# Linear attention into a sine-gated feed-forward layer: where the attention output products stand, how batch 2's q is transposed, and how the last output block is cut

## The chip, the cores and the metric

The kernel runs on one core of one Trainium2 chip. The metric is the device time of one execution in microseconds (us). A core has a matrix engine (PE, with its weight loads shown as PEld), a vector engine (DVE), a scalar engine (ACT), a general engine (POOL) and a sync engine (SP), which here only issues DMAs. Each engine works through its own instructions in order; engines wait for one another by semaphores. Matrix products land in PSUM, and DVE or ACT must copy a result out ("evict" it) before its PSUM tile can be used again.

## What is computed

Attention without a score matrix: q is a softmax over the head dimension, k a softmax over the sequence, and the output of a head is q times (k transposed times v). The result, 4608 tokens of 512 numbers, goes through a layer with 2048 hidden units.

```python
# q, k, v: (8 batches, 8 heads, 576 tokens, 64)
q_s = softmax(q, axis=-1)
k_s = softmax(k, axis=2)
kv  = einsum('bhsd,bhse->bhde', k_s, v)
x   = einsum('bhsd,bhde->bhse', q_s, kv)      # then to (4608, 512)
h   = x @ w_in                                # (4608, 2048)
s   = sin(alpha * h)
g   = h + s * s / (alpha + 1e-09)
out = g @ w_out                               # (4608, 512)
```

## The kernel before

**Two tilings.** Attention goes by batch: 8 batches of 576 tokens, each token index cut into 9 groups (J = 9) of 64 (P). The layer goes by token tiles of 512: 9 tiles, numbered t = 0 to 8. Tile t + 1 needs tokens of batch t + 1 at the latest, so the attention of batch t + 1 is done while tile t is worked, for t = 3 to 6; batch 3 is done while tile 2 is worked. "Stage t" below is the loop over the 16 hidden blocks ni of tile t.

**The layer.** `mm_h` (L235) makes one hidden block: four products (ki = 0 to 3) over the 512 inputs into a PSUM tile hp, 128 x 512. `sine` (L241 to L247) takes the sine on ACT and the square on ACT, POOL or DVE, by a letter in a string. `combine` (L251) writes g on DVE and frees hp. `o_stream` is a generator: each `take(os, n)` issues n products g x w_out (L255) of the tile before, 64 for a tile, 16 for each of four output blocks; after each 16 `evac_o` copies the block (L261) and stores it in two halves (L264).

**The attention of a batch.** exp of q and k on ACT (L114), row sums on DVE (L136, L137), the division on POOL or DVE, into qn (L143); qn is transposed into qT by a DMA on SP (`q_transpose_dma`, L202). `kv_mm` (L154) makes the 64 x 64 products of k and v with 36 small products, `kv_norm` (L164, L167) divides them on DVE into kbd. `attn_out(b, ii, half, pool, eng)` multiplies kbd with qT for one half ii of the heads and one part of the token groups (groups 0 to 3, or 4 to 8): two products (L212) into one tile xp, and one copy (L215) into xT, the input of `mm_h`. Four calls of it make a batch. Calls are counted 0 to 3 below, in the order (ii 0, first part), (ii 0, second part), (ii 1, first part), (ii 1, second part).

**PSUM.** From stage 2 on: ps_h has four tiles (hp), ps_o two (op, lent to hp in stage 2), and ps_a one, which kvp and xp share. So in ps_a each product waits until the tile's last content was copied out.

**The order.** All is written out by hand in the order of issue; nothing is moved by a scheduler. In stages 2 to 6 `attn_back(b, ni - 5)` is called once a block: at ni = 5 it makes kv, at ni = 10, 11, 12, 13 one call of attn_out each. In stage 2 the copies alternate between ACT and DVE and the combine lags two blocks behind; in stages 3 to 6 the copies are all on DVE and `q_transpose_dma` stands at ni = 4, behind it on SP the stores of the output blocks. `load_batch` queues the q, k and v loads of a later batch on SP.

**Batch 2** is done before stage 2, among the output products of tile 1. Its q is transposed in two DMAs, one for each ii. Its products are made in another form: four products of six token groups (`attn_chunk`, L220), each into a tile of ps_h, and four of three groups into one tile of ps_a; the six groups are the 384 tokens that tile 2 needs. The copies (L440, L445) are two on ACT and three on DVE.

**The tail.** The last output block is made in two parts of 256 columns (L498), each copied on DVE and stored in two halves, one from SP's queue and one from ACT's.

Of the kernel before, what the change touches and what calls it, by code (L numbers as in the profile page):

```python
# [15 lines left out]
F32 = mybir.dt.float32  # L16
# [7 lines left out]
def kernel(  # L24
# [14 lines left out]
    nc = tc.nc  # L39
    ctx.enter_context(nc.allow_non_contiguous_dma(reason="layout"))  # L40
    B, H, S, D = q.shape
    dm = H * D
    d_ff = moe_w_in.shape[1]
    NT = B * S
    J = 9
    P = S // J
    nN = d_ff // 128
    MF = 512
    nT = NT // MF
# [17 lines left out]
    xT = singles.tile([128, 4, NT], BF16, name="xT")  # L67
    win = singles.tile([128, 4, d_ff], BF16, name="win")
    wout = singles.tile([128, nN, dm], BF16, name="wout")
# [6 lines left out]
    def src_view(t, b):  # L76
        return t[b].rearrange("(i e) (p j) d -> (e p) i (j d)", e=2, j=J)
# [7 lines left out]
    def load(name, t, b, halves=False, eng=nc.sync):  # L85
        st = stage.tile([128, 4, J, D], F32, name=f"st_{name}", tag="st")
        view = src_view(t, b)
        flat = st.rearrange("p i j d -> p i (j d)")
        if halves:
            for ii in range(2):  # L90
                eng.dma_start(out=flat[:, ii::2], in_=view[:, ii::2])
        else:
            eng.dma_start(out=flat, in_=view)
        staged[name, b] = st
# [15 lines left out]
    A = {}  # L110
# [14 lines left out]
    def cast_v(b, engs):  # L125
        vv = vb[b % 2].rearrange("p j (i c) -> p i j c", i=4)
        for ii in range(2):
            engs[ii](vv[:, 2 * ii:2 * ii + 2, :, 0:D], staged["v", b][:, ii::2])  # L128

    def norm_q(b, engs):  # L130

        qe = A["qe", b].rearrange("p j (ii x d) -> p ii j x d", ii=2, x=2)
        A["qn", b] = qn = att1.tile([128, 2, J, 2 * D], BF16, name="qn")
        qs = small.tile([128, J, 4], F32, name="qs")
        if len(engs) == 1:
            nc.vector.tensor_reduce(qs, A["qe", b].rearrange("p j (i d) -> p j i d", i=4), axis=AXL.X, op=ALU.add)  # L136
            nc.vector.reciprocal(qs, qs)  # L137
        for ii in range(2):
            part = qs[:, :, 2 * ii:2 * ii + 2]
            if len(engs) == 2:  # L140
                nc.vector.tensor_reduce(part, qe[:, ii], axis=AXL.X, op=ALU.add)
                nc.vector.reciprocal(part, part)
            engs[ii % len(engs)].tensor_tensor(qn[:, ii].rearrange("p j (x d) -> p j x d", x=2), qe[:, ii],  # L143
                                               part.unsqueeze(3).to_broadcast([128, J, 2, D]), op=ALU.mult)
# [27 lines left out]
    def q_tile(b):  # L172
        if ("qT", b) not in A:
            A["qT", b] = att2.tile([128, 2, J, 128], BF16, name="qT")
        return A["qT", b]
# [15 lines left out]
        for j in range(j0, j1):  # L191
            nc.tensor.transpose(tp[:, j - j0], A["qn", b][:, ii, j], identb)

    def q_transpose_dma(b, halves=False):
        for ii in range(2) if halves else (slice(0, 2),):
            out, in_ = q_tile(b)[:, ii], A["qn", b][:, ii]
            if not halves:
                out, in_ = out.rearrange("p ii j c -> p (ii j) c"), in_.rearrange("p ii j c -> p ii (j c)")
                in_ = in_.rearrange("p ii c -> p (ii c)")
            else:  # L200
                in_ = in_.rearrange("p j c -> p (j c)")
            nc.sync.dma_start(out=out, in_=in_, transpose=True)  # L202

    XO = ((0, 4), (4, 9))

    def attn_out(b, ii, half, pool, eng):
        qT, kt = A["qT", b], kbd[b % 2]
        j0, j1 = XO[half]
        n = (j1 - j0) * P
        xp = pool.tile([128, 2, 512], F32, name="xp", tag="a")  # L210
        for e in range(2):
            nc.tensor.matmul(xp[:, e, 0:n], kt[:, e, ii], qT[:, ii, j0:j1, e * 64:(e + 1) * 64],  # L212
                             start=True, stop=True)
        c0 = (J * b + j0) * P
        eng(xT[:, 2 * ii:2 * ii + 2, c0:c0 + n], xp[:, :, 0:n])  # L215

    def attn_chunk(b, c, j0, j1, xp):

        ii, e = divmod(c, 2)
        nc.tensor.matmul(xp, kbd[b % 2][:, e, ii], A["qT", b][:, ii, j0:j1, e * 64:(e + 1) * 64],  # L220
                         start=True, stop=True)


    G = {}
# [29 lines left out]
    def mm_o(t, j, ni, acc):  # L254
        nc.tensor.matmul(acc, G[t][:, ni, j * 128:(j + 1) * 128], wout[:, ni, :],  # L255
                         start=(ni == 0), stop=(ni == nN - 1))

    def evac_o(t, j, acc, eng, cols=None, queues=None):
        cols = cols or slice(0, dm)
        o = opool.tile([128, dm], F32, name="o")  # L260
        eng(o[:, cols], acc)  # L261
        for hf in range(2):
            blk = t * BPT + 2 * j + hf
            (queues or (nc.sync, nc.sync))[hf].dma_start(out=out_v[blk // J, blk % J][:, cols],  # L264
                                                         in_=o[64 * hf:64 * hf + 64, cols])


    ACT_CP, DVE_CP, GP_CP = nc.scalar.copy, nc.vector.tensor_copy, nc.gpsimd.tensor_copy
# [6 lines left out]
    for ii, j0, j1 in VJ:  # L275
        nc.sync.dma_start(out=st[:, ii::2, j0:j1].rearrange("p i j d -> p i (j d)"),
                          in_=src_view(v, 0)[:, ii::2, j0 * D:j1 * D])
# [48 lines left out]
    ps_h = ctx.enter_context(tc.tile_pool(name="ps_h", bufs=4, space=PSUM, reuse_waits="tile"))  # L326
# [5 lines left out]
    def flush(lag, keep):  # L332
        while len(lag) > keep:
            combine(*lag.pop(0))

    def o_quad(t, accs, engs):

        R = range(4)
        orders = [[(n, m) for p in (0, 2) for n in R for m in (p, p + 1)],
                  [(n, m) for n in R for m in R], [(n, m) for n in R for m in R],  # L340
                  [(n, m) for m in R for n in R]]
        for c in R:
            for n, m in orders[c]:
                mm_o(t, m, 4 * c + n, accs[m])
                if c == 3 and n == 3:
                    evac_o(t, m, accs[m], engs[m])
                yield

    def take(it, n=1000):
        for _ in range(n):  # L350
            if next(it, 0) == 0:
                return
# [4 lines left out]
    with tc.tile_pool(name="ps_e", bufs=2, space=PSUM, reuse_waits="tile") as ps_e:  # L357
# [4 lines left out]
        for ni in range(nN):  # L362
            h_slot(0, ni, "PAPDPAPADPAPPDAP"[ni], lag, lent)
            flush(lag, 1)
            if ni in late:
                name, x, b, hv = late[ni]
# [12 lines left out]
        os = o_quad(0, accs, [DVE_CP, ACT_CP, DVE_CP, ACT_CP])  # L379
# [24 lines left out]
    ps_o = ctx.enter_context(tc.tile_pool(name="ps_o", bufs=2, space=PSUM, reuse_waits="tile"))  # L404
    ps_a = ctx.enter_context(tc.tile_pool(name="ps_a", bufs=1, space=PSUM, reuse_waits="tile"))


    def o_stream(t, eng=DVE_CP):
        for j in range(4):
            acc = ps_o.tile([128, dm], F32, name="op", tag="o")  # L410
            for ni in range(nN):
                mm_o(t, j, ni, acc)
                if ni == nN - 1:
                    evac_o(t, j, acc, eng)
                yield
# [4 lines left out]
    os = o_stream(1)  # L420
# [2 lines left out]
    exp_q(3)  # L423
    exp_k(3)
    load("v", v, 3)
    q_transpose_dma(2, halves=True)
    cast_v(3, [GP_CP, GP_CP])
    nc.scalar.activation(zero, zero, AX.Sin)
    take(os, 16)
# [1 line left out]
    kv_mm(2, 1, ps_a)  # L431
    kv_norm(2)
    norm_q(3, [GP])
    take(os, 20)

    c0 = J * 2 * P
    for c in range(4):
        xp = ps_h.tile([128, MF], F32, name="hp", tag="h")[:, 0:6 * P]
        attn_chunk(2, c, 0, 6, xp)
        (ACT_CP, DVE_CP)[c % 2](xT[:, c, c0:c0 + 6 * P], xp)  # L440
        take(os, 1)
    xp = ps_a.tile([128, 2, 512], F32, name="xp", tag="a")[:, :, 0:6 * P]
    for c in range(4):
        attn_chunk(2, c, 6, 9, xp[:, c // 2, (c % 2) * 3 * P:(c % 2 + 1) * 3 * P])
    DVE_CP(xT[:, :, c0 + 6 * P:c0 + 9 * P].rearrange("p (h c) n -> p h c n", h=2),  # L445
           xp.rearrange("p h (c n) -> p h c n", c=2))
    take(os)
    q_transpose_dma(3)
    load_batch(4)

    def attn_back(b, n, engs=(DVE_CP, DVE_CP)):
        if n == 0:
            kv_mm(b, 0, ps_a)
            kv_mm(b, 1, ps_a)
            kv_norm(b)
        elif 5 <= n < 9:
            attn_out(b, (n - 5) // 2, (n - 5) % 2, ps_a, engs[n % 2])

    def lent():
        return ps_o.tile([128, MF], F32, name="op", tag="o")  # L460
# [2 lines left out]
    for ni in range(nN):  # L463
        h_slot(2, ni, SQ2[ni], lag, lent)
        flush(lag, 2)
        attn_back(3, ni - 5, (DVE_CP, ACT_CP))
    flush(lag, 0)

    for t in range(3, nT):
        b = t + 1 if t + 1 < B else None  # L470
        os = o_stream(t - 1)
        done = 0
        for ni in range(nN):
            hp = mm_h(t, ni)
# [15 lines left out]
            done = min(64, want)  # L490
        take(os)

    take(o_stream(nT - 1), 48)
    for h in range(2):
        cols = slice(h * 256, h * 256 + 256)
        acc = ps_o.tile([128, 256], F32, name="op", tag="o")
        for ni in range(nN):
            nc.tensor.matmul(acc, G[nT - 1][:, ni, 384:512], wout[:, ni, cols], start=(ni == 0), stop=(ni == nN - 1))  # L498
        evac_o(nT - 1, 3, acc, DVE_CP, cols, (nc.sync, nc.scalar))


# [1 line left out]
_INS = ['q', 'k', 'v', 'moe_w_in', 'moe_w_out', 'moe_alpha']  # L503
_OUTS = [((4608, 512), 'float32')]
# [25 lines left out]
```

## Time and profile before

| | us |
|---|---|
| median of 3 runs | 293.47 (293.15 to 294.47) |
| the profiled execution | 293.15 |
| its span, first to last instruction | 291.4 |
| granted clock of the matrix engine | 1.00 |
| stage 2, first product to first product of stage 3 | 79.85 to 96.92 |
| stage 3, the same | 96.92 to 127.36 |
| stages 4, 5, 6, the same | 127.36, 157.72, 188.08, 218.60 |
| stage 7 and stage 8, without attention | 218.60 to 246.22, 246.22 to 272.99 |
| the last block's products | from 284.21 |

The span is what the profiler sees between the first and the last instruction; the time has 1.75 us more around it. Stage times are read from the start of the first product of tile t in the chain and the timeline, except 96.92, which is the start of the twelve products at 95.19 plus eight at 0.216. A row of a timeline gives the start, the duration, the engine, the line and what it does; in brackets stands how long the engine was idle before and who ended the wait.

### The profile page before, as it was taken

Reading aid. Unit: us, or ns where it says so; the run is one execution under the profiler, and the core shown is the slowest. Engines: PE = TensorE matmul, PEld = TensorE weight load, DVE = VectorE, ACT = ScalarE, POOL = GpSimd, SP = SyncE. Lnnn points to the kernel's source line nnn. Section 1 sums busy time; section 2 is a strip of 40 time slices with the busy share of each in tenths; the row PEclk is TensorE's granted clock in tenths of the full one; section 3 lists DMA queues with packets and bytes.
Section 4 is the critical chain, followed back from the end, with each engine's and each line's share of the span. In section 5 each row is a group of like instructions: output and inputs, shape, how many; then the busy total and the mean of one; then the engine's idle time right before and its main releaser. Section 6 shows DMA issues by size and latency. Waiting matters only on the chain.

```text
span 291.4 us, 4261 instructions
## 1 busy us (share of the span) xinstructions
PE 278.9 (96%) x1576; PEld 132.4 (45%) x1576; DVE 188.0 (65%) x275; ACT 226.7 (78%) x320; POOL 84.9 (29%) x78
## 2 busy tenths in 40 slices
PE   2999999999999999999999999999999999999994
PEld 1444445444454445444444444445444444444444
DVE  3748955798958667855786568756774555555412
ACT  4679956999579899789987998799977777777500
POOL 0939571576684744002600070005000000000000
PEclk9999999999999999999999999999999999999999
DMA  7999999964899975109920894113411111111143
GB/s 260 294 181 207 357 254 339 395 226 130 208 139 374 393 239 117 37 23 334 290 55 14 290 292 97 36 39 70 83 38 36 36 36 38 36 36 37 38 108 73
DMA packets 35253, 45.77 MB, mean 157 GB/s; under 512 B 15888, under 2 KB 19744, under 8 KB 35232
## 3 DMA queue, kind: packets, MB, share of 16 engines
q1 hardware_dynamic: 29632, 34.09, 41.3%
q0 software_dynamic: 5408, 11.27, 15.4%
q8 instruction: 12, 0.20, 0.3%
q10 hardware_dynamic: 192, 0.14, 0.2%
q14 instruction: 9, 0.07, 0.1%
HBM read 36.71 MB, written 9.44 MB: 158 GB/s over the span
## 4 chain that ended last, share of the span: by engine, by line
PE 80%; DVE 8%; ACT 5%; POOL 3%; issue 2%; DMA 1%; ACTq 0%
PE op L255 35%; PE hp L235 31%; PE hp L255 4%; DVE g L251 3%; PE warm L299 2%; PE kvp L154 2%; POOL s L245 2%; DVE xT L215 2%; ACT s L241 2%; PE xp L212 2%; DMA st_q<-in_q_dram 1%; PE op L498 1%; PE hh L235 1%; ACT s L243 1%; DVE o L261 1%
## 5 line engine op out<-in xcount | busy, mean ns | idle before, releaser
L251 DVE SCALAR_TENSOR_TENSOR g<-s,inva_sb,hp 128x512 bf16<-128x512 f32 x130 | 95.3, 746 | 64.6 <-ACT s L243 52.1
L235 PE MATMUL hp<-xT,win 128*128 128x512 bf16 x520 | 129.5, 379 | 0.2
L255 PE MATMUL op<-wout,g 128*128 128x512 bf16 x496 | 124.0, 379 | 0.0
L241 ACT ACTIVATE s<-hp,alpha_sb 128x512 f32<-128x512 f32 x130 | 87.8, 682 | 29.4 <-PE hp L235 25.4
L235 PEld LDWEIGHTS <-win 128*128 128x128 bf16 x576 | 56.1, 98 | 68.1 <-issue 1.9
L255 PEld LDWEIGHTS <-g 128*128 128x128 bf16 x560 | 54.1, 98 | 62.6 <-issue 1.5
L243 ACT ACTIVATE s<-s 128x512 f32<-128x512 f32 x112 | 70.5, 629 | 3.6
L143 POOL TENSOR_TENSOR qn<-qe,qs 128x1152 bf16<-128x1152 bf16 x13 | 27.4, 2127 | 83.7 <-DVE qs L137 67.6
L245 POOL TENSOR_TENSOR s<-s 128x512 f32<-128x512 f32 x27 | 28.4, 1058 | 23.6 <-ACT s L241 23.4
L261 DVE COPY o<-op 128x512 f32<-128x512 f32 (+1 forms) x33 | 21.9, 664 | 10.1 <-PE op L255 7.6
L114 ACT ACTIVATE ke<-st_k 128x1152 bf16<-128x1152 f32 x16 | 17.7, 1149 | 3.2 <-DMA st_k<-in_k_dram 3.2
L114 ACT ACTIVATE qe<-st_q 128x1152 bf16<-128x1152 f32 x16 | 17.9, 1156 | 2.9 <-DMA st_q<-in_q_dram 2.9
L136 DVE TENSOR_REDUCE qs<-qe 128x36 f32<-128x2304 bf16 x5 | 12.8, 2553 | 10.8 <-ACT qe L114 10.7
L128 POOL CAST vb<-st_v 128x1152 bf16<-128x1152 f32 x14 | 16.1, 1175 | 8.7 <-DMA st_v<-in_v_dram 8.6
L215 DVE CAST xT<-xp 128x512 bf16<-128x512 f32 (+1 forms) x22 | 16.5, 752 | 2.8 <-PE xp L212 2.7
L255 PE MATMUL hp<-wout,g 128*128 128x512 bf16 x64 | 15.1, 379 | 0.4 <-DVE g L251 0.3
L212 PE MATMUL xp<-qT,kbd 128*128 128x256 bf16 (+1 forms) x56 | 10.8, 285 | 2.1 <-DVE xT L215 1.0
L154 PE MATMUL kvp<-vb,ke 64*128 64x130 bf16 x288 | 9.8, 216 | 0.5 <-ACT qT L187 0.4
L114 ACT ACT_TABLE_LOAD x7 | 9.0, 1283 | 1.3 <-PEq L514 1.2
L154 PEld LDWEIGHTS <-ke 64*128 64x128 bf16 x288 | 8.2, 93 | 3.8 <-issue 2.1
L299 PE MATMUL warm<-qe,identb 128*128 128x512 bf16 x19 | 7.4, 554 | 2.7 <-ACT qe L114 2.7
L212 PEld LDWEIGHTS <-kbd 128*128 128x128 bf16 x56 | 5.3, 97 | 9.2 <-issue 3.8
(59 smaller groups left out, 121.3 us busy)
## 6 DMA issues: line engine op xcount, KB each, us to landing
out_dram<-o SPq DMA_DIRECT2D x70, 128.0 KB, 2.4
st_q<-in_q_dram SPq DMA_DIRECT2D x5, 1152.0 KB, 6.1
st_k<-in_k_dram SPq DMA_DIRECT2D x5, 1152.0 KB, 8.7
st_v<-in_v_dram SPq DMA_DIRECT2D x5, 1152.0 KB, 10.9
st_k<-in_k_dram POOLq DMA_DIRECT2D x2, 1152.0 KB, 11.1
wout<-in_moe_w_out_dram POOLq DMA_DIRECT2D x4, 512.0 KB, 14.6
st_q<-in_q_dram SPq DMA_DIRECT2D x2, 576.0 KB, 4.4
st_k<-in_k_dram SPq DMA_DIRECT2D x2, 576.0 KB, 7.1
```

The costliest lines, as they stand in the source:

```text
L114: nc.scalar.activation(dst[:, :, ii * 128:(ii + 1) * 128].rearrange("p j (x d) -> p x j d", x=2), src[:, ii::2], AX.Exp)
L143: engs[ii % len(engs)].tensor_tensor(qn[:, ii].rearrange("p j (x d) -> p j x d", x=2), qe[:, ii], part.unsqueeze(3).to_broadcast([128, J, ...
L154: nc.tensor.matmul(kvp[:, e, ii * 130:(ii + 1) * 130], ke[r, j, ii * 128:(ii + 1) * 128], vt[r, j, ii * 130:(ii + 1) * 130], start=(j == 0 ...
L212: nc.tensor.matmul(xp[:, e, 0:n], kt[:, e, ii], qT[:, ii, j0:j1, e * 64:(e + 1) * 64], start=True, stop=True)
L215: eng(xT[:, 2 * ii:2 * ii + 2, c0:c0 + n], xp[:, :, 0:n])
L235: nc.tensor.matmul(hp, win[:, ki, ni * 128:(ni + 1) * 128], xT[:, ki, t * MF:(t + 1) * MF], start=(ki == 0), stop=(ki == 3))
L241: nc.scalar.activation(s, hp, AX.Sin, scale=alpha_sb[:, ni:ni + 1])
L243: nc.scalar.activation(s, s, AX.Square)
L245: nc.gpsimd.tensor_tensor(s, s, s, op=ALU.mult)
L251: nc.vector.scalar_tensor_tensor(G[t][:, ni], in0=s, scalar=inva_sb[:, ni:ni + 1], in1=hp, op0=ALU.mult, op1=ALU.add)
L255: nc.tensor.matmul(acc, G[t][:, ni, j * 128:(j + 1) * 128], wout[:, ni, :], start=(ni == 0), stop=(ni == nN - 1))
L261: eng(o[:, cols], acc)
```

## The change

Three things change. First, batch 2: its q is transposed by one DMA, and its products are made by four calls of `attn_out` in the one tile of ps_a, with all copies on ACT. Six more output products (26 for 20) stand ahead of them, and 2, 2, 1 and 1 behind them. Second, `attn_back` gets a list of places: the four calls stand at ni = 8, 10, 12, 14 in stages 3 to 6 and at ni = 9, 11, 13, 15 in stage 2, where the copies now go DVE, ACT, DVE, ACT instead of ACT, DVE, ACT, DVE. Third, the last block is cut into 352 and 160 columns.

```diff
-    def q_transpose_dma(b, halves=False):
-        for ii in range(2) if halves else (slice(0, 2),):
...
-            nc.sync.dma_start(out=out, in_=in_, transpose=True)
+    def q_transpose_dma(b):
+        nc.sync.dma_start(out=q_tile(b).rearrange("p ii j c -> p (ii j) c"),
+                          in_=A["qn", b].rearrange("p ii j c -> p (ii j c)"), transpose=True)
...
-    q_transpose_dma(2, halves=True)
+    q_transpose_dma(2)
...
-    take(os, 20)
-
-    c0 = J * 2 * P
-    for c in range(4):
-        xp = ps_h.tile([128, MF], F32, name="hp", tag="h")[:, 0:6 * P]
-        attn_chunk(2, c, 0, 6, xp)
-        (ACT_CP, DVE_CP)[c % 2](xT[:, c, c0:c0 + 6 * P], xp)
-        take(os, 1)
-    xp = ps_a.tile([128, 2, 512], F32, name="xp", tag="a")[:, :, 0:6 * P]
-    for c in range(4):
-        attn_chunk(2, c, 6, 9, xp[:, c // 2, (c % 2) * 3 * P:(c % 2 + 1) * 3 * P])
-    DVE_CP(xT[:, :, c0 + 6 * P:c0 + 9 * P].rearrange("p (h c) n -> p h c n", h=2),
-           xp.rearrange("p h (c n) -> p h c n", c=2))
-    take(os)
+    take(os, 26)
+    for n in range(4):
+        attn_out(2, n // 2, n % 2, ps_a, ACT_CP)
+        take(os, (2, 2, 1, 1000)[n])
...
-    def attn_back(b, n, engs=(DVE_CP, DVE_CP)):
+    def attn_back(b, n, engs=(DVE_CP, DVE_CP), xs=(3, 5, 7, 9)):
...
-        elif 5 <= n < 9:
-            attn_out(b, (n - 5) // 2, (n - 5) % 2, ps_a, engs[n % 2])
+        elif n in xs:
+            m = xs.index(n)
+            attn_out(b, m // 2, m % 2, ps_a, engs[m % 2])
...
-        attn_back(3, ni - 5, (DVE_CP, ACT_CP))
+        attn_back(3, ni - 5, (DVE_CP, ACT_CP), (4, 6, 8, 10))
...
-    for h in range(2):
-        cols = slice(h * 256, h * 256 + 256)
-        acc = ps_o.tile([128, 256], F32, name="op", tag="o")
+    for c0, c1 in ((0, 352), (352, 512)):
+        acc = ps_o.tile([128, dm], F32, name="op", tag="o")[:, 0:c1 - c0]
```

More of the change, by code (lines that the diff above doesn't have):

```diff
@@ L192, in q_transpose_ii @@
             nc.tensor.transpose(tp[:, j - j0], A["qn", b][:, ii, j], identb)
-    def q_transpose_dma(b, halves=False):
-        for ii in range(2) if halves else (slice(0, 2),):
[L196 to L202, printed above, removed]
+    def q_transpose_dma(b):
+        nc.sync.dma_start(out=q_tile(b).rearrange("p ii j c -> p (ii j) c"),
+                          in_=A["qn", b].rearrange("p ii j c -> p (ii j c)"), transpose=True)
     XO = ((0, 4), (4, 9))
@@ L493 @@
     take(o_stream(nT - 1), 48)
-    for h in range(2):
-        cols = slice(h * 256, h * 256 + 256)
-        acc = ps_o.tile([128, 256], F32, name="op", tag="o")
+    for c0, c1 in ((0, 352), (352, 512)):
+        acc = ps_o.tile([128, dm], F32, name="op", tag="o")[:, 0:c1 - c0]
         for ni in range(nN):
-            nc.tensor.matmul(acc, G[nT - 1][:, ni, 384:512], wout[:, ni, cols], start=(ni == 0), stop=(ni == nN - 1))
-        evac_o(nT - 1, 3, acc, DVE_CP, cols, (nc.sync, nc.scalar))
+            nc.tensor.matmul(acc, G[nT - 1][:, ni, 384:512], wout[:, ni, c0:c1], start=(ni == 0), stop=(ni == nN - 1))
+        evac_o(nT - 1, 3, acc, DVE_CP, slice(c0, c1), (nc.sync, nc.scalar))
 _INS = ['q', 'k', 'v', 'moe_w_in', 'moe_w_out', 'moe_alpha']
```

## The prediction

> **What bounds the kernel now.** I read the page's busy times first, then the chain that ended last, then the timeline of three places that the change touches, one after the other: the block in which batch 2's attention output is made, stage 3 (token tiles are counted from 0; stage t works the first product of tile t), and the last four microseconds. "ni" numbers the 16 blocks of the hidden dimension inside a stage.
>
> ```profile
> PE 278.9 (96%) x1576; PEld 132.4 (45%) x1576; DVE 188.0 (65%) x275; ACT 226.7 (78%) x320; POOL 84.9 (29%) x78
> ...
> PE 80%; DVE 8%; ACT 5%; POOL 3%; issue 2%; DMA 1%; ACTq 0%
> ```
>
> The matrix engine is busy 96% of the span and is 80% of the chain. So a change pays only where it takes a gap out of PE, and costs whatever gap it puts in. One stage in the table of windows (columns: span of the window, then busy time and count of PE, PEld, DVE, ACT, POOL):
>
> ```profile
> 127.36:157.72 30.36, 30.10 (x173) 14.22 (x172) 20.60 (x29) 27.19 (x39) 6.48 (x4) 1.00 0.60 171
> ```
>
> Stages 3 to 6 each repeat in 30.36 us. DVE has 9.8 us to spare there, PE almost nothing. Now the block of batch 2 (timeline of PE: start, duration, instruction):
>
> ```profile
> 71.61 4.49 PE L255 MATMUL op<-wout,g 128*128 128x512 bf16 x20
> 76.10 0.32 PE L220 MATMUL hp<-qT,kbd 128*128 128x384 bf16 x1
> ...
> 78.12 1.89 PE L255 MATMUL op<-wout,g 128*128 128x512 bf16 x8
> 79.85 0.38 PE L235 MATMUL hp<-xT,win 128*128 128x512 bf16 x1
> ```
>
> From 76.10 to 79.85 PE does 12 output products at 0.216 (16 of them take 3.46 in the chain), four attention products of 384 columns (0.16) and four of 192 (0.08): 2.59 + 0.64 + 0.33 = 3.56 of 3.75 us. The old form has 0.2 us of gap.
>
> **Part 1: batch 2.** The old form used four separate PSUM tiles of the pool ps_h and one of ps_a, so no product waited for an eviction. The new form makes four calls of attn_out, all in ps_a, which has one tile, all evicted by ACT. Each call must wait until ACT has emptied the tile. What such a hop costs is seen in stage 2, where the same function runs with ACT:
>
> ```profile
> 94.29 0.58 ACT L215 CAST xT<-xp 128x512 bf16<-128x512 f32 x1
> ...
> 94.92 0.43 PE L212 MATMUL xp<-qT,kbd 128*128 128x320 bf16 x2
> ```
>
> The next product starts 0.05 after the eviction ends (94.87 to 94.92). ACT was busy with a sine before it; where the evicting engine is free it starts 0.41 after the first product of 256 columns (47.59 to 48.00) and 0.47 for 320 (94.92 to 95.39, DVE). So hops are 0.41 + 0.58 + 0.05 = 1.04 and 0.47 + 0.69 + 0.05 = 1.21 (0.69 is the longest 640-element eviction on ACT, 0.697). ACT is free in the block: it stood idle 3.04 us before stage 2's first sine. The first product of stage 2 reads xT from all four calls: its first two weight blocks (ki 0, 1) need calls 0 and 1, the other two calls 2 and 3. From the first call (T0) to the moment the third weight block can run: 1.04 + 1.21 + 1.04 + 1.21 = 4.50, so the stage starts in effect at T0 + 4.50 - 0.43 = T0 + 4.07. Six output products are between and after the calls; they are the cover and are too few.
>
> T0 also waits for the transposed q. The two DMAs of 9 blocks become one of 18, which needs both halves of qn; the second (DVE, 70.93 + 1.97) ends at 72.90, so SP issues it near 73.0. Landings of all seven issues:
>
> ```profile
> DMA to landing us min/median/max: 3.8/4.6/5.6
> ```
>
> The halves took 4.3 and 3.8; the whole ones 4.6 to 5.6, and 4.6 where loads don't share the queue, which holds here (the v load of batch 3 has landed by 74.9). So it lands at 77.6. Add 0.1 for the wake-up (first half: landed 76.01, product 76.10) and 0.2 because the weight load itself now waits (weight load to product, 97.57 to 97.78): T0 = 77.9. PE would be there at 71.61 + 26 x 0.216 = 77.23, so 0.7 us of it is DMA. Stage 2 starts at 77.9 + 4.07 = 81.97 in place of 79.85: **+2.1**. Bounds: landing in time (T0 77.23) gives +1.45; 5.6 to land gives T0 78.9, +3.1. What stands behind the transpose on SP are output stores, whose o tiles (4 buffers) nobody needs before stage 3. On ACT the four evictions stand ahead of stage 2's first sine, which needs the same products anyway. On DVE three evictions go away, which frees nothing that PE waits for. The Trainium skill (DMA: Bandwidth & Descriptors, section Anatomy of one DMA) has a fixed part of about 2.0 us in each DMA, and its section Latency and other measured facts gives 261 GB/s for a transpose: 590 KB would land in 4.3 us, as an estimate from that page, and the block would cost 1.8. This case's whole transposes were never that quick. Trace Analysis, section Matmuls, wants independent products to rotate through PSUM banks so that evictions overlap; it speaks against this part: by it a form with a tile for each call would pay nothing here, and the sum of all parts would be 295.2 in place of 297.3.
>
> **Part 2: stage 2 (batch 3).** The four calls go from ni 10, 11, 12, 13 to ni 9, 11, 13, 15, with DVE and ACT changing places. Old gaps on PE: 91.66 to 92.37, 93.50 to 93.72, 94.80 to 94.92 = 1.04. New: call 0 after ni 9 (89.72); its DVE eviction stands behind the combine of ni 7 (90.40 to 91.15), so it is done at 91.85 and call 1 waits 0.25 after ni 11. Call 2 finds its tile free. Call 3 comes after ni 15, directly ahead of stage 3's first product, whose third weight block needs its result: ACT must do ni 14's sine and square and ni 15's sine before it, and is done near 97.9, while PE stands ready at 96.5. That product ends at 98.35 instead of 97.78: **+0.6**. The gaps are moved to the stage's end, not removed. Bounds: all 1.04 gained; or 1.0 lost if ACT runs a square later.
>
> **Part 3: stages 3 to 6 (batches 4 to 7).** Calls go from ni 10, 11, 12, 13 to ni 8, 10, 12, 14; call 0 stood at 148.12. The stage of batch 5:
>
> ```profile
> 140.78 3.41 SPq L202 DMA_TRANSPOSE qT<-qn  x1
> ...
> 145.32 0.81 PE L255 MATMUL op<-wout,g 128*128 128x512 bf16 x3
> ...
> 150.56 1.03 PE L235 MATMUL hp<-xT,win 128*128 128x512 bf16 x4
> ...
> 151.84 0.38 PE L212 MATMUL xp<-qT,kbd 128*128 128x256 bf16 x2 [0.26 <-DVE xT L215]
> ```
>
> The old gap is the one before call 2: 150.56 + 4 x 0.216 = 151.42 to 151.84, 0.42 us. With two slots (some 2.8 us) between calls, a DVE eviction of 0.68 or 0.82 is over in time: the gap goes, 4 x 0.42 = **-1.7**. But call 0 moves to where PE now stands at 145.32, and the transpose, issued at 140.78 when POOL ends qn, took 5.4 and landed at 146.2. The four stages: issue 110.32, 140.78, 171.20, 201.56; landing after 4.6, 5.4, 5.6, 4.6, at 114.92, 146.18, 176.80, 206.16; PE there at 114.96, 145.32, 175.68, 206.03. With 0.3 to wake, the new waits are 0.26 + 1.16 + 1.42 + 0.43 = **+3.3**. All of PE's queue stands behind each wait. The chain to the landing (sine of ni 0, exp on ACT, sum on DVE, qn on POOL, DMA) starts with the stage, so a later stage doesn't outrun it. Net **+1.6**. Bounds: all land after 3.8, before PE comes: -1.7; all after 5.6: 5.5 - 1.7 = +3.8. The eviction placed earlier on DVE costs nothing, hidden by the 9.8 us of spare; without that cover it is 0.7 a stage.
>
> **Part 4: the tail.**
>
> ```profile
> 286.00 0.42 DVE L261 COPY o<-op 128x256 f32<-128x256 f32 x1 [1.06 <-PE op L498]
> 287.74 0.42 DVE L261 COPY o<-op 128x256 f32<-128x256 f32 x1 [1.32 <-PE op L498]
> ```
>
> PE's 32 products have the same columns in all. The last copy shrinks from 256 to 160 columns: 512 cost 0.69 and 256 cost 0.42, so 0.10 less; its store is 40 KB in place of 64. **-0.1** (0 to -0.3). The larger first piece is copied by 287.2 and is stored before the second.
>
> **Sum.** 2.1 + 0.6 + 1.6 - 0.1 = +4.2 on the profiled execution's 293.15 (span 291.4, 1.75 around it): 297.35, given as 297.3. That execution is the lowest of three; the median is 0.3 above.
>
> **Rivals.** (a) The transposes land early: after 3.8, as the quickest half did, everywhere. Then the spread pays its 1.7 and batch 2 costs only 1.45: 1.45 + 0.6 - 1.7 - 0.1 = +0.3, 293.4, not slower. It decides from a landing below about 4.2. Against it: no whole transpose was under 4.6. (b) Stage 2 absorbs the block, because POOL's qn, which held back the first square until 81.93, and the ACT lag no longer count: only the 1.6 and part of the rest stay, near 295.2. Against it: PE runs 79.85 to 90.58 almost without a gap, so nothing can be caught up. (c) Every landing takes 5.6: 3.1 + 0.6 + 3.8 - 0.1 = +7.4, 300.5. For it: batch 6; against it: two stages at 4.6. (d) The spread does not take the old gap away, since evictions queue behind combines on DVE: +1.7 more, 299.0; against it the 9.8 us.
>
> **How the numbers follow.** Forecast (295.6 to 298.6) 0.60; (a) 0.10, (b) 0.14, (c) 0.06, (d) 0.10. Range 294.7 to 299.2, leaving (c) and most of (a) out. About 0.5% is what a measurement can tell from no change: 292.0 to 294.9 counts as the same. Slower 0.88, same 0.08, faster 0.04, the last two from (a) and the low edge of (b).
>
> **What would show it.** After the change: call 0 in stages 4 and 5 waits over 0.8 us for a DMA and call 2 waits for nothing; between the first call of batch 2 and stage 2's first product some 4 us with three waits for ACT; a gap over 0.5 us inside stage 3's first product; the other stages (7, 8) unchanged. No DMA wait at ni 8, or stage 2 starting less than 1 us later, would make the prediction wrong.

## The result and the profile after

| | us |
|---|---|
| before, median of 4 runs | 293.87 (293.15 to 294.47) |
| changed, median of 4 runs | 297.22 (296.42 to 297.44) |
| ratio, 95% interval | 1.011 (1.0078 to 1.0143) |
| the profiled execution of the changed kernel, its span | 297.31, 295.5 |

The kernel before has one more run here than in the table ahead of the prediction. The changed kernel is slower by 1.1% (0.8 to 1.4), some 3.2 us; 297.3 was forecast. From the profile of the changed kernel: busy times, chain, and the group of the attention products (busy time, mean ns of one, idle time before them and what ended it):

```profile
PE 278.4 (94%) x1576; PEld 131.4 (44%) x1576; DVE 185.9 (63%) x272; ACT 228.5 (77%) x322; POOL 85.8 (29%) x78
...
PE 68%; DMA 14%; DVE 7%; ACT 4%; POOL 3%; issue 2%; SPq 1%; ACTq 0%; DVEq 0%; POOLq 0%
...
L206 PE MATMUL xp<-qT,kbd 128*128 128x256 bf16 (+1 forms) x64 | 12.4, 285 | 4.2 <-DMA qT<-qn 1.6
```

The same group before the change:

```profile
L212 PE MATMUL xp<-qT,kbd 128*128 128x256 bf16 (+1 forms) x56 | 10.8, 285 | 2.1 <-DVE xT L215 1.0
```

PE does the same work and its share fell from 96% to 94%: idle time was added. PE now stands idle 4.2 us ahead of the attention products, where it was 2.1. The chain holds DMAs, 14% of it, where it held PE; a weight load of the start is among them.

The block of batch 2 in the timeline of the changed kernel (start, duration, instruction, in brackets idle time and releaser):

```profile
73.82 2.94 SPq L195 DMA_TRANSPOSE qT<-qn  x1
...
79.29 0.38 PE L206 MATMUL xp<-qT,kbd 128*128 128x256 bf16 x2 [1.04 <-DMA qT<-qn]
...
80.35 0.43 PE L206 MATMUL xp<-qT,kbd 128*128 128x320 bf16 x2 [0.24 <-ACT xT L209]
...
81.56 0.38 PE L206 MATMUL xp<-qT,kbd 128*128 128x256 bf16 x2 [0.35 <-ACT xT L209]
...
82.61 0.43 PE L206 MATMUL xp<-qT,kbd 128*128 128x320 bf16 x2 [0.46 <-ACT xT L209]
...
83.82 3.18 PE L229 MATMUL hp<-xT,win 128*128 128x512 bf16 x14
```

One wait for the DMA and three for ACT, and the third weight block of stage 2 starts at 83.82, 4.53 us after the first call. Then the end of stage 2 and the beginning of stage 3:

```profile
99.32 0.44 PE L206 MATMUL xp<-qT,kbd 128*128 128x320 bf16 x2
99.87 0.59 PE L229 MATMUL hp<-xT,win 128*128 128x512 bf16 x2
101.22 0.59 PE L229 MATMUL hp<-xT,win 128*128 128x512 bf16 x2 [0.75 <-ACT xT L209]
```

Stage 3's first product stops in its middle until ACT has copied the last call's result. And the stages of batches 5 and 6:

```profile
144.24 3.37 SPq L195 DMA_TRANSPOSE qT<-qn  x1
...
149.55 0.38 PE L206 MATMUL xp<-qT,kbd 128*128 128x256 bf16 x2 [0.61 <-DMA qT<-qn]
...
155.64 0.38 PE L206 MATMUL xp<-qT,kbd 128*128 128x256 bf16 x2
...
180.58 0.38 PE L206 MATMUL xp<-qT,kbd 128*128 128x256 bf16 x2 [0.94 <-DVE g L245]
```

Call 2 (155.64) has no bracket any more; call 0 has one. In the second stage the profile names DVE's combine, which ends at 180.44; the transpose, issued at 175.01, landed 5.43 us later, at 180.45. Which of the two it was is settled by an experiment below.

The chain is best compared by marks that all kernels have: the first k-v product of batches 2, 3 and 4, the first product of the last block, and the span's end. All are read from the profiles, in us. The left column is the time of the first mark, the others are distances to the next. (The last block's first product starts at 284.05 in the timeline of the kernel before; the 284.21 of the earlier table is where the chain enters it.)

| kernel | k-v of batch 2 at | to k-v of 3 (block) | to k-v of 4 (stage 2) | to last block (stages 3 to 8) | to the end |
|---|---|---|---|---|---|
| before | 70.48 | 14.65 | 24.37 | 174.55 | 7.32 |
| changed | 71.34 | 17.32 | 24.62 | 175.05 | 7.18 |
| changed, second profile | 71.92 | 17.30 | 24.61 | 174.47 | 7.17 |

The changes of the four parts are +2.67, +0.25, +0.50 (-0.08 in the second profile) and -0.14 (-0.15). The other 0.86 of the 4.1 us between the two spans lies before anything that was changed.

### The profile page after: what moved, and what is told of

It reads as the page before. It is cut to its first block, busy times and chain, and to the rows that moved or that the text cites. A ratio compares the mean times of both kernels' runs of the same rounds, so it can differ in the third digit from the quotient of the medians.

```text
span 295.5 us, 4265 instructions
## 1 busy us (share of the span) xinstructions
PE 278.4 (94%) x1576; PEld 131.4 (44%) x1576; DVE 185.9 (63%) x272; ACT 228.5 (77%) x322; POOL 85.8 (29%) x78
## 4 chain that ended last, share of the span: by engine, by line
PE 68%; DMA 14%; DVE 7%; ACT 4%; POOL 3%; issue 2%; SPq 1%; ACTq 0%; DVEq 0%; POOLq 0%
PE hp L229 29%; PE op L249 26%; DMA win<-in_moe_w_in_dram 4%; PE hp L249 4%; DMA qT<-qn 4%; DMA st_v<-in_v_dram 3%; PE xp L206 3%; DVE g L245 2%; DMA out_dram<-o 2%; PE kvp L154 2%; PE hh L229 2%; ACT s L235 1%; DVE qs L141 1%; DMA st_q<-in_q_dram 1%; PE op L483 1%
## 5 line engine op out<-in xcount | busy, mean ns | idle before, releaser
L235 ACT ACTIVATE s<-hp,alpha_sb 128x512 f32<-128x512 f32 x130 | 87.7, 682 | 27.6 <-PE hp L229 27.2
L255 DVE COPY o<-op 128x512 f32<-128x512 f32 (+2 forms) x33 | 21.9, 663 | 14.1 <-PE op L249 11.8
L128 POOL CAST vb<-st_v 128x1152 bf16<-128x1152 f32 x14 | 17.0, 1244 | 8.4 <-DMA st_v<-in_v_dram 8.4
L206 PE MATMUL xp<-qT,kbd 128*128 128x256 bf16 (+1 forms) x64 | 12.4, 285 | 4.2 <-DMA qT<-qn 1.6
L209 ACT CAST xT<-xp 128x640 bf16<-128x640 f32 (+1 forms) x10 | 6.5, 658 | 7.1 <-PE xp L206 7.0
L229 PE MATMUL hh<-xT,win 128*128 128x512 bf16 x40 | 9.4, 379 | 0.9 <-DMA win<-in_moe_w_in_dram 0.9
```

What stands on the lines that cost most here:

```text
L229: nc.tensor.matmul(hp, win[:, ki, ni * 128:(ni + 1) * 128], xT[:, ki, t * MF:(t + 1) * MF], start=(ki == 0), stop=(ki == 3))
L235: nc.scalar.activation(s, hp, AX.Sin, scale=alpha_sb[:, ni:ni + 1])
```

## The experiments

Each was compared with the kernel before on the same chip; the line numbers in profiles are those of the experiment's own code, and "before" is 294.3 to 294.4 in these comparisons.

### The block alone

```diff
-    q_transpose_dma(2, halves=True)
+    q_transpose_dma(2)
...
+    take(os, 26)
+    for n in range(4):
+        attn_out(2, n // 2, n % 2, ps_a, ACT_CP)
+        take(os, (2, 2, 1, 1000)[n])
```

> The kernel before with only the new form of batch 2 (one DMA for q, four calls in the one tile, all copies on ACT). Theory: the block alone is the loss. From the end of batch 2's kv products to the third weight block of stage 2 it takes 2.7 us longer than before (8.2 to 10.9), the time is 2.5 to 2.9 us above before, and stages 2 to 6 keep their old lengths. Rival 1 (the spread is what costs): under 1 us above before. Rival 2 (stage 2 catches the delay up): the block is 2.7 longer but stage 3 begins less than 2 us later, relative to the block's start.

Measured: 297.11, ratio 1.0096 (1.0079 to 1.0113). Block 17.31, stage 2 24.38, stages 3 to 8 174.55: the block is 2.66 longer and every later distance is the old one to 0.01. The block alone is about the whole loss; rivals 1 and 2 are out. The old gap in stage 2 is still there, at full length, though the stage began 2.7 us late (the first row is the block's first call; the last is stage 2's second call, and behind it the same call before the change):

```profile
79.34 0.38 PE L212 MATMUL xp<-qT,kbd 128*128 128x256 bf16 x2 [1.03 <-DMA qT<-qn]
...
95.96 0.43 PE L212 MATMUL xp<-qT,kbd 128*128 128x320 bf16 x2 [0.55 <-ACT xT L215]
```

```profile
92.37 0.43 PE L212 MATMUL xp<-qT,kbd 128*128 128x320 bf16 x2 [0.55 <-ACT xT L215]
```

### The block's two costs: the changed kernel with two transposes; the old kernel with one

```diff
-    q_transpose_dma(2)
+    q_transpose_dma(2, halves=True)
```

> The changed kernel with batch 2's q transposed in two halves again. Theory: call 0 no longer waits for the DMA (the first half lands about 1 us before PE is there, the second before call 2), the four hops stay at 4.5 us; 1.0 to 1.2 us below the changed kernel, 2.0 to 2.4 above before. Rival 1 (the wait for the DMA and the hops overlap, the hops alone set the end): no gain. Rival 2 (the DMA is nearly all of it): more than 2 us below the changed kernel.

Measured: 295.87, ratio 1.0056 (1.0041 to 1.0071). Block 16.12. The first call of the block starts at 78.38 without a wait, and the hops stay:

```profile
78.38 0.38 PE L212 MATMUL xp<-qT,kbd 128*128 128x256 bf16 x2
79.44 0.43 PE L212 MATMUL xp<-qT,kbd 128*128 128x320 bf16 x2 [0.24 <-ACT xT L215]
```

So of the block's 2.66 us the hops through the one tile are 16.12 - 14.65 = 1.5, and the late q 1.2. The new form also has all its copies on ACT; no run separates that from the single tile, but ACT's copies are not the longer ones (0.58 and 0.69 here; DVE takes 0.68 and 0.82 for the same sizes). The time above before, 1.5 us between the medians, is less than the theory's 2.0 to 2.4.

> The kernel before with only batch 2's q transposed by one DMA instead of two halves; products, tiles and copies as before. Theory: the one transpose is issued 1.2 us after the first half was and lands 5.3 us later, so the first product waits 2.0 to 2.5 us, nothing else is late, and the time is 2 to 2.4 above before: in the changed kernel the six output products put ahead hide 1.3 of this. Rival (the DMA's lateness matters only through the single tile): under 0.5 above.

The edit is the opposite one, in the kernel before. Measured: 296.19, ratio 1.0069 (1.0047 to 1.0092). Block 16.66, 2.0 longer, all other distances as before:

```profile
79.06 0.32 PE L220 MATMUL hp<-qT,kbd 128*128 128x384 bf16 x1 [2.20 <-DMA qT<-qn]
```

One transpose for two costs 2.0 us where the products come at the old place; in the changed kernel, with six output products put ahead of them, the late q costs 1.2. The rival is out.

### The spread alone, in stages 3 to 6

```diff
+    def attn_back(b, n, engs=(DVE_CP, DVE_CP), xs=(3, 5, 7, 9)):
...
+        attn_back(3, ni - 5, (ACT_CP, DVE_CP), (5, 6, 7, 8))
```

The second line keeps stage 2 as it was.

> The kernel before with only the four calls of stages 3 to 6 moved to ni 8, 10, 12, 14. Theory: gap before call 2 gone (0.4 a stage) and waits of call 0 for the transposed q of 0.1, 0.8, 1.1 and 0.2 in place of it; stages 3 and 6 shorter by 0.3 to 0.4, stages 4 and 5 longer by 0.3 and 0.7; in all 0 to +0.6. Rival 1 (the terms as forecast): +1.6. Rival 2 (the waits of the changed kernel are an effect of its late stage 2): no wait at call 0 and -1.7.

Measured: 294.22, ratio 0.9996 (0.9983 to 1.001). Stages 3 to 8 take 174.71, 0.16 more than before; call 0 waits 0.54 and 0.64 for the transpose in stages 4 and 5, and call 2 for nothing. Gain and loss cancel; neither the +1.6 of the forecast nor a gain of 1.7.

### The same, with q transposed in halves

```diff
-                    q_transpose_dma(b)
+                    q_transpose_dma(b, halves=True)
```

> The spread of stages 3 to 6 alone (ni 8, 10, 12, 14), with q of batches 4 to 7 transposed in two halves, the first issued when POOL has done the first half of qn (2.1 us earlier). Theory: the landing of the whole transpose is what call 0 waits for; the first half lands before PE comes, the waits of 0.7 and 0.8 in stages 4 and 5 go, the gap before call 2 stays away: 1.4 to 1.7 us below before. Rival 1 (call 0 waits for DVE's combines, which the profile names in one stage): the waits stay, time as before. Rival 2 (halves land no earlier, since the loads fill the queue): waits halve, 0.7 below.

Measured: 293.97, ratio 0.9985 (0.9973 to 0.9997); stages 3 to 8 take 173.63, 0.92 less. That is less than the theory's 1.4 to 1.7. Call 0 in stages 4 and 5:

```profile
146.32 0.38 PE L212 MATMUL xp<-qT,kbd 128*128 128x256 bf16 x2
...
177.01 0.38 PE L212 MATMUL xp<-qT,kbd 128*128 128x256 bf16 x2 [0.59 <-DMA qT<-qn]
```

In stage 4 the wait is gone although three combines still run on DVE from 145.21 to 147.29, past the product's start: call 0 does not wait for combines (rival 1 is out, and the bracket in the changed kernel named the wrong one). In stage 5 the wait stays and the stage is 0.7 us longer than the one before it: the first half was issued at 169.69 and took 7.2 us (rival 2 in that stage). The next batch's k and v loads were in flight with it; but they were with stage 4's first half too, for about as long, and that one landed after 5.7. In stages 3 and 6, with no load in flight, a half took 3.2. What made stage 5's so late is not shown.

### Later places for the same spread

```diff
-    def attn_back(b, n, engs=(DVE_CP, DVE_CP), xs=(3, 5, 7, 9)):
+    def attn_back(b, n, engs=(DVE_CP, DVE_CP), xs=(4, 6, 8, 10)):
```

> The spread of stages 3 to 6 alone, one slot later: ni 9, 11, 13, 15. Theory: PE reaches call 0 about 1.3 us later, when the whole transpose has landed (waits under 0.2 a stage) and the gap before call 2 is gone: 1.3 to 1.7 us below before, if the eviction of call 3 is done before the next stage's first product asks for it. Rival (the place of the last call is the new limit): a wait of 0.3 to 0.8 for DVE's xT in the next stage's first product, 0 to 0.5 below before.

Measured: 292.96, ratio 0.9944 (0.9924 to 0.9964); stages 3 to 8 take 172.88, 1.67 less, and stage for stage 29.94 from k-v products to k-v products where it was 30.36. Call 0 and call 2 in stage 4, neither with a bracket:

```profile
147.80 0.38 PE L212 MATMUL xp<-qT,kbd 128*128 128x256 bf16 x2
...
153.90 0.38 PE L212 MATMUL xp<-qT,kbd 128*128 128x256 bf16 x2
```

One slot decides: the spread is worth its 4 x 0.42 when call 0 stands behind the landing. The rival's wait at the stage's end did not come.

> The spread of stages 3 to 6 alone at ni 9, 11, 12, 14. Theory: call 0 waits for nothing; between calls 1 and 2 there is one slot of 1.5 us for an eviction chain of 1.34 us, and the copy of an output block on DVE (0.69) falls into it, so a gap of 0.2 to 0.5 a stage stays: as before, to 0.8 below. Rival (any two slots between calls 0 and 1 are enough): 1.5 below.

With xs=(4, 6, 7, 9) the time was 295.41, ratio 1.0039 (1.0026 to 1.0051), and stages 3 to 8 took 175.43, 0.88 more. A gap was expected, but not one longer than the old. DVE and PE between calls 1 and 2:

```profile
151.90 0.68 DVE L261 COPY o<-op 128x512 f32<-128x512 f32 x1
...
152.50 0.81 DVE L215 CAST xT<-xp 128x640 bf16<-128x640 f32 x1
...
153.37 0.38 PE L212 MATMUL xp<-qT,kbd 128*128 128x256 bf16 x2 [0.47 <-DVE xT L215]
```

The copy of an output block comes first on DVE and holds back call 1's eviction. PE's slot ended at 152.73 (151.87 and four products), so PE loses 0.64 us. A call one slot later is not safer by itself; what counts is what stands ahead on DVE.

### The spread alone, in stage 2

```diff
+        attn_back(3, ni - 5, (DVE_CP, ACT_CP), (4, 6, 8, 10))
```

> The kernel before with only the four calls of stage 2 moved to ni 9, 11, 13, 15 (and DVE and ACT changing places). Theory: the three gaps of 1.0 us inside the stage go, and a wait of 0.8 to 1.0 for ACT comes inside stage 3's first product; the stage is 0 to 0.6 us longer. Rival (the gaps are simply removed): 1 us shorter.

Measured: 294.84, ratio 1.0012 (0.9998 to 1.0025); stage 2 takes 24.62, 0.25 more. The gaps inside go, and the new one is where the theory put it:

```profile
99.54 0.38 PE L235 MATMUL hp<-xT,win 128*128 128x512 bf16 x1 [0.76 <-ACT xT L215]
```

### The changed kernel with the old block, and the changed kernel again

The first of these undoes the block only.

> The changed kernel with only batch 2's block as before (two halves, the tiles of ps_h). Theory: +0.33 from stage 2, 0 to +0.25 from stages 3 to 6, -0.2 from the tail: 0 to 0.4 above before, and 2.5 to 3.0 below the changed kernel run beside it. Rival (the parts interact: without the late block the waits grow): more than 1 us above before.

> The changed kernel again, on the same chip as the others. Theory: 2.7 (block) + 0.3 (stage 2) + 0 to 0.25 (stages 3 to 6) - 0.2 (tail) = 2.8 to 3.1 above before; the first comparison's profile was 4.1 longer because its stage 0 waited 0.9 us for a weight load, which comes and goes in kernels that are the same up to there. Rival (that wait belongs to the change): 3.7 to 4.2 above before.

Measured: the old block gives 294.78, ratio 1.0 (0.9985 to 1.0015), with distances of 14.72, 24.61, 174.35 and 7.12. The changed kernel gives 297.26, ratio 1.0094 (1.0074 to 1.0113). The block is worth 2.5 us between the two, and the other three parts together nothing that can be measured. The changed kernel is 2.8 above before, as the theory has it; the rival's 3.7 to 4.2 is out. Stage 0 of kernels that are the same up to there (the changed kernel, then the spread of stage 2 alone):

```profile
25.20 1.89 PE L229 MATMUL hh<-xT,win 128*128 128x512 bf16 x8 [0.86 <-DMA win<-in_moe_w_in_dram]
```

```profile
25.99 1.89 PE L235 MATMUL hh<-xT,win 128*128 128x512 bf16 x8 [1.49 <-DMA win<-in_moe_w_in_dram]
```

This wait was absent in the profile of before and in four of the experiments. The k-v products of batch 2 began between 70.48 and 72.13 in all profiles; that of before, against which the forecast's sum was made, had the earliest start of all. It has no wait here, and it also came to these products at 19.10, where the other four without the wait came at 19.83 to 19.95.

### Versions that beat both

> The kernel before with the calls of stages 3 to 6 at ni 9, 11, 13, 15 and the last block cut into 352 and 160. Theory: -1.7 and -0.2, 1.6 to 2.0 below before. Rival (the tail's cut is worth nothing): as the spread alone, the time from the last block's first product to the end stays 7.3 us in place of 7.2.

Measured: 293.01, ratio 0.994 (0.9917 to 0.9962), distances of 14.70, 24.37, 172.88 and 7.11: the tail's cut is worth 0.2, which the ratio can't show.

```diff
-        attn_back(3, ni - 5, (ACT_CP, DVE_CP), (5, 6, 7, 8))
+        attn_back(3, ni - 5, (DVE_CP, ACT_CP), (4, 6, 8, 9))
```

> The same, and the calls of stage 2 at ni 9, 11, 13, 14 with copies on DVE, ACT, DVE, ACT. Theory: the gaps inside stage 2 go, and the wait of stage 3's first product for the last copy on ACT falls from 0.8 to 0.3 or 0.4: stage 2 about 0.1 shorter than before, the time 0 to 0.3 below the version with stage 2 as before. Rival (a call after ni 14 queues behind that block's square on ACT and costs as much): no gain or 0.3 longer.

Measured: 292.05, ratio 0.9918 (0.9897 to 0.9939), the lowest median of all, though its interval overlaps those of the last version and of the later places alone; stage 2 takes 24.03, 0.34 less than before, more than expected. The wait in stage 3's first product fell to 0.18:

```profile
96.11 0.43 PE L212 MATMUL xp<-qT,kbd 128*128 128x320 bf16 x2
...
98.16 0.38 PE L235 MATMUL hp<-xT,win 128*128 128x512 bf16 x1 [0.18 <-ACT xT L215]
```

Of the 0.96 between the last two medians stage 2 explains 0.34. The two profiles differ by another 0.81 ahead of the first mark (72.09 and 71.28), where nothing was changed; stage 0 of the first has a wait of 0.92 for the weight load, the second none.

## Why the prediction came out, and where its terms did not

The direction, the place and the mechanisms held. The total fits better than its terms: their sum was +4.2, and the parts that were changed came to +3.3 and +2.7 in two profiles. That 297.3 came so near to 297.2 is luck to about 1 us: parts 2 and 3 were put too high, part 1 too low, the sum of them about 1 us too high, and it was added to an execution with an early start.

**Part 1 (+2.1): measured +2.67.** The hops were forecast as 4.50 and took 4.53. Mis-sized was the landing: 4.6 us was taken because the v load "has landed by 74.9", but the forecast's own issue, at 73.0, comes before that. In the changed kernel the v load landed 5.8 after its issue at 69.99 and the transpose was issued at 73.82, so both were in flight for 2 us, and the transpose landed after 5.3 (5.30 to 5.34 in all four profiles that have it). From the landing to the product passed 0.13, not 0.3. Counted as in the forecast (72.47 and 26 products give 78.09, and the first call starts at 79.29) PE waited 1.2 in place of 0.7, which is the difference between +2.67 and +2.1; the bracket's 1.04 counts from the end of the last product.

**Part 2 (+0.6): measured +0.25.** The gaps moved to the stage's end as said. ACT's last copy was done 0.3 earlier than worked out.

**Part 3 (+1.6): measured +0.50 and -0.08.** The gain of 4 x 0.42 was right, as the later spread shows (1.67). The waits were forecast as 0.26, 1.16, 1.42, 0.43. In the changed kernel call 0 starts 0.11, 0.77, 1.10 and 0.22 after PE is free (in stage 4, 147.91 and four products give 148.78, and it starts at 149.55): 2.2 in place of 3.3. From landing to product passed 0.13 to 0.14 in all four, not the 0.3 that was put together from two rows. The landings were 0.2 earlier in two stages as well. In the second profile batches 5 and 6 landed after 5.02 and 4.99 where they took 5.17 and 5.43 in the first; that is the difference between -0.08 and +0.50.

**Part 4 (-0.1): measured -0.14 and -0.15.** The last copy takes 0.32 as worked out.

**The signs.** Call 2 waits for nothing, the block shows three waits for ACT and 3.8 us from its first call to stage 2's first product, and stage 3's first product stops for 0.75; stage 7 kept its length (27.6). Call 0 was late by 1.10 in stage 5 but by 0.77 in stage 4, just under the 0.8 that was named.

**The rivals.** Landing early (a) did not happen: no whole transpose took less than 4.55. Stage 2 did not absorb the block (b): after the block alone its length was the old one to 0.01. Late landings (c) came in the first profile for batches 2, 3, 5 and 6 (5.2 to 5.7), not for 4 and 7 (4.6). The gap before call 2 (d) did go.

The rule that independent groups of products should rotate through different PSUM banks, so that copying one out overlaps the next (the Trainium skill, Perfetto Trace Analysis, section Matmuls), agrees with the block: four calls through one tile cost 1.5 us, and in the old form, with a tile for each product of six groups, no product waited for a copy. No run tried the four new calls with a tile each.

The estimate of 4.3 us for a whole transpose, from the page DMA: Bandwidth & Descriptors, was below all that were measured, but by little where no load was in flight: 4.55 to 4.61. With a load in flight they took 4.68 to 5.65. The 2.0 us in it are fitted there to DMAs issued by the general engine (POOL), while these are issued by SP, and the 261 GB/s stand there for a transpose with a non-contiguous middle dimension.

## What to carry to other kernels

Moving a consumer earlier to spread work is worth only what its latest input allows: look up the landing of each input in the trace, and place the first consumer behind it; here one slot turned nothing into 1.7 us. Products that go through a single PSUM tile need as much other work between them as product and eviction take (1.0 to 1.2 us here), counted with what stands ahead in the evicting engine's queue. Splitting a DMA in two paid where its first half had a consumer of its own and landed in time (2.0 us in batch 2 of the old form); in one stage here the half came too late, among loads, and nothing was gained.

## What the hardware showed that was not expected

A transpose's landing goes with what else is in flight. All whole transposes of batches 4 and 7, with no load in flight, took 4.55 to 4.61 us, in every profile; all other whole ones had a load in flight for part of their time and took 4.68 to 5.65. With no load in flight a half took 3.20 to 3.26, so by these two sizes some 1.9 us of a transpose do not go with its bytes (an estimate: twice 3.23 less 4.58, the means). And one half, queued among loads, landed after 7.2 us, later than any whole one.

The start of a kernel varies more between executions than most of the parts studied: the mark before the block moved by 1.65 us between profiles of kernels that are the same up to there, with a wait for a weight load of 0 to 1.5 us in it.
